# SBUF tiles on 512-byte lines, and constant products ahead of chunk 4's transposes

## The chip, the cores and the metric

The kernel runs on one core of one Trainium2 chip. The metric is the device time of one execution in microseconds; where several runs are shown, their median counts. A core has TensorE (PE; its weight loads are listed as PEld), VectorE (DVE), ScalarE (ACT), GpSimd (POOL) and SyncE (SP), which work in their own order and wait for each other through semaphores. Sixteen DMA engines move data between HBM and SBUF; a transfer is issued by SP, ACT or POOL and stands in that engine's DMA queue.

## The reference, cut to what matters

First a linear attention with decay per head, then a feed-forward layer with a leaky activation:

```python
gamma = 1.0 - 2.0 ** (-5.0 - np.arange(H))            # B=4, H=8, S=768, D=64
for t in range(S):
    state = gamma[None, :, None, None] * state + einsum('bhd,bhe->bhde', k[:, :, t], v[:, :, t])
    y[:, :, t] = scale * einsum('bhd,bhde->bhe', q[:, :, t], state)
x = y.transpose(0, 2, 1, 3).reshape(B * S, H * D)      # 3072 x 512
h = x @ w_in                                           # 512 x 2048
g = maximum(h, 0) + alpha * minimum(h, 0)
out = g @ w_out                                        # 2048 x 512
```

## The kernel before

The recurrence is done in chunks of 128 time steps. A batch has 6 chunks, so there are 24 chunks, numbered u; four chunks make one block of 512 tokens, and there are 6 blocks n. A chunk goes through these steps:

- `load(u)` (line 101): SP issues three transfers, k, q and v of the chunk, 256 KB each, in runs of 256 bytes (64 floats of one head), each into its own SBUF tile. Eight buffers of each.
- `prep(u)`: k times a decay table goes into the fp16 tile kdq (line 119; on DVE for chunks 0 to 7, later on POOL), q times another into its other half (line 127, POOL), and v is cast to fp16 into one of eight tiles vext (line 139, POOL). vext has, for each of four pairs of heads, three blocks of 64 columns: the first head's v, zeros, the second head's v. From chunk 10 on (`NPE`) a DMA transposes kdq into kq.
- `stage_a(u)`: for chunks 0 to 9 PE transposes kdq, eight transposes into the PSUM tile trb (line 156), of which the first four need k and the last four q; ACT copies them to kq (line 163). Unless it is a batch's last chunk, PE makes the state's update stp from kdq and vext (line 169), DVE adds it to the state (line 181, or copies it for a batch's first chunk, line 185), and POOL scales the state into tg (line 187).
- `stage_b(u)`: PE makes the scores sca and scb, pairs of products on 64 rows each (line 202); DVE masks them (line 212).
- `stage_c(u)`: PE makes the outputs yps (lines 227, 234, 242), ACT copies them to xT (line 252), the block's transposed input to the feed-forward layer.

`ffn1(n)` makes 16 products hps of 512 columns (line 270), each of four matmuls, whose activation is done by ACT (line 280) and DVE (line 281); `ffn2(n)` makes the block's outputs ops (line 309), which ACT copies (line 318) and stores. Both are generators: `tick(gen, m)` lets the next m matmuls be issued.

The order on each engine is as the program writes it (`manual_schedule`). Chunks 0 to 3 come first. The weights, w_in in four parts and w_out in four, are issued by POOL in between (lines 348 and 352), with a cast from float32 to fp16. The loads of chunks 4 to 11 are issued by SP once the second part of w_out has landed (`held`). Then `ffn1(0)` runs, then 19 matmuls of `ffn2(0)`, with `prep(4)` before the last nine, and then chunks 4 to 7 are interleaved with the rest of `ffn2(0)`:

```python
    gen = ffn2(0, parts=4)
    tick(gen, 10)
    prep(4)
    tick(gen, 9)
    for u in range(UB, 2 * UB):
        stage_a(u)
        tick(gen, 5)
        if u > UB:
            stage_c(u - 1)
```

Later blocks run `ffn1(n)`, and `ffn2(n)` interleaved with the four chunks of the next block.

PSUM has eight buffers of one bank, four under the tag `pa` (chunks, and every second product of ffn1(0) from the fifth on) and four under `pb`; a tag's buffers are taken in turn. SBUF tiles lie one behind the other in the order in which they are first named: tab, mi, alpha, warm, oma, w_in, w_out, the eight vext, the states, and then those of chunks and blocks.

Of the kernel before, what the change touches and what calls it, by code (L numbers as in the profile page):

```python
# [9 lines left out]
FP = mybir.dt.float32  # L10
F16 = mybir.dt.float16
# [7 lines left out]
def kernel(  # L19
# [10 lines left out]
    nc = tc.nc  # L30
    B, H, S, D = q.shape
    d_model, d_ff = moe_w_in.shape
    NFT = d_ff // 128
    NP = H // 2
# [9 lines left out]

    NTAB = 2 * H + NP + 16
    tab_np = np.zeros((128, NTAB), dtype=np.float64)
    for h in range(H):
        tab_np[:, h] = g64[h] ** (127.0 - p_ar)  # L50
        tab_np[:, H + h] = scale * g64[h] ** (p_ar + 1.0 - 128.0)
    for p in range(NP):
        tab_np[0:64, 2 * H + p] = g64[2 * p] ** 128
        tab_np[64:128, 2 * H + p] = g64[2 * p + 1] ** 128
    tab_np[0:NFT, NTAB - 16 : NTAB] = np.eye(NFT)
    tab_np = tab_np.astype(np.float32)
# [7 lines left out]
    sbp = ctx.enter_context(tc.tile_pool(name="sbp", bufs=1, space=bass.MemoryType.SB))  # L64
    psp = ctx.enter_context(tc.tile_pool(name="psp", bufs=1, space=bass.MemoryType.PSUM))
    ctx.enter_context(tc.manual_schedule())

    tab = sbp.tile([128, NTAB], FP, tag="tab", name="tab")
    mi = sbp.tile([128, 256], F16, tag="mi", name="mi")
    mask = mi[:, 0:128]  # L70
    ident = mi[:, 128:256]
    alpha_sb = sbp.tile([NFT, 128], FP, tag="alpha", name="alpha")
    warm = sbp.tile([128, 1], FP, tag="warm", name="warm")
    oma_sb = sbp.tile([128, NFT], FP, tag="oma", name="oma")
    w_in_all = sbp.tile([128, 4, d_ff], F16, tag="win", name="win")
    w_out_all = sbp.tile([128, NFT, d_model], F16, tag="wout", name="wout")


    NV = 8
    NPE = 10  # L80
    vext = [sbp.tile([128, NP, 3, 64], F16, tag=f"vx{i}", name=f"vx{i}") for i in range(NV)]

    NT = 2
    sst = [sbp.tile([128, NP, 128], FP, tag=f"ss{i}", name=f"ss{i}") for i in range(NT)]
# [2 lines left out]
    def ps(name, dt=FP, n=512, tag="pa"):  # L87
        return psp.tile([128, n], dt, tag=tag, bufs=4, name=name)
# [27 lines left out]
    def prep(u, between=None):  # L116
        t = staged.pop(u)
        kdq = sbp.tile([128, 2, H, D], F16, tag="kdq", bufs=8, name=f"kdq{u}")
        (nc.vector if u < 2 * UB else nc.gpsimd).tensor_tensor(  # L119
            out=kdq[:, 0],  # L120
            in0=t["k"],
            in1=tab[:, 0:H].unsqueeze(2).to_broadcast([128, H, D]),
            op=MULT,
        )
        if between:
            between()
        nc.gpsimd.tensor_tensor(  # L127
            out=kdq[:, 1],
            in0=t["q"],
            in1=tab[:, H : 2 * H].unsqueeze(2).to_broadcast([128, H, D]),  # L130
            op=MULT,
        )
        kq = sbp.tile([128, 2 * NP, 128], F16, tag="kq", bufs=8, name=f"kq{u}")
        if u >= NPE:
            nc.sync.dma_start_transpose(
                out=kq, in_=kdq.rearrange("p a h d -> p (a h d)")
            )
        vx = vext[u % NV]
        nc.gpsimd.tensor_copy(  # L139
            out=vx[:, :, 0::2, :],  # L140
            in_=t["v"].rearrange("p (a b) d -> p a b d", b=2),
        )
        prepped[u] = (kdq, kq, vx)
# [52 lines left out]
    def stage_b(u):  # L196
        kq, vx = live[u]
        scs = [ps("sca"), ps("scb")]
        for p in range(NP):
            for lh in range(2):  # L200
                s = slice(64 * lh, 64 * lh + 64)
                nc.tensor.matmul(  # L202
                    out=scs[lh][:, 128 * p : 128 * p + 128],
                    lhsT=kq[s, 128 * p : 128 * p + 128],
                    rhs=kq[s, 512 + 128 * p : 512 + 128 * p + 128],
                    start=True,
                    stop=True,
                )
        m2s = []
        for lh in range(2):  # L210
            m2 = sbp.tile([128, NP, 128], F16, tag=f"m2{lh}", bufs=2, name=f"m2{lh}")
            nc.vector.tensor_tensor(  # L212
                out=m2,
                in0=scs[lh].rearrange("p (a i) -> p a i", i=128),
                in1=mask.unsqueeze(1).to_broadcast([128, NP, 128]),
                op=MULT,
            )
            m2s.append(m2)
        live[u] = (kq, vx, m2s)

    def stage_c(u):
        b, c = divmod(u, NCH)
        kq, vx, m2s = live.pop(u)
        yps = ps("yps")
        for p in range(NP):
            o = yps[:, 128 * p : 128 * p + 128]
            nc.tensor.matmul(  # L227
                out=o,
                lhsT=vx[:, p, 0:2, :].rearrange("p a d -> p (a d)"),
                rhs=m2s[0][:, p, :],  # L230
                start=True,
                stop=False,
            )
            nc.tensor.matmul(  # L234
                out=o,
                lhsT=vx[:, p, 1:3, :].rearrange("p a d -> p (a d)"),
                rhs=m2s[1][:, p, :],
                start=False,
                stop=(c == 0),
            )  # L240
            if c > 0:
                nc.tensor.matmul(  # L242
                    out=o,
                    lhsT=tgs[u][:, p, :],
                    rhs=kq[:, 512 + 128 * p : 512 + 128 * p + 128],
                    start=False,
                    stop=True,
                )
        n, i = divmod(u, UB)
        if i == 0:  # L250
            xT[n] = sbp.tile([128, NP, TB], F16, tag="xT", bufs=2, name=f"xT{n}")
        nc.scalar.activation(  # L252
            out=xT[n][:, :, C * i : C * i + C],
            in_=yps.rearrange("p (a i) -> p a i", i=128),
            func=COPY,
            bias=0.0,
            scale=1.0,
        )
# [41 lines left out]
    def ffn2(n, parts=1):  # L300
# [3 lines left out]
        for f0 in range(0, NFT, step):  # L304
            for tq in range(UB):
                if f0 == 0:
                    opss[tq] = ps("ops", tag="pb")
                for ft in range(f0, f0 + step):
# [13 lines left out]
                        nc.scalar.dma_start(out=out[row : row + 128, :], in_=os_sb)  # L322
                    yield

    def tick(gen, m):
        for _ in range(m):
            if next(gen, 1) == 1:
                return
# [27 lines left out]
    for u in range(UB):  # L356
# [3 lines left out]
        if u == 0:  # L360
            aps = ps("aps")
            nc.tensor.transpose(
                out=aps[:, 0:NFT], in_=alpha_sb, identity=tab[0:NFT, NTAB - 16 : NTAB]
            )
        stage_b(u)
        if u == 0:
            nc.vector.tensor_scalar(
                out=oma_sb, in0=aps[:, 0:NFT], scalar1=-1.0, scalar2=1.0, op0=MULT, op1=ADD
# [12 lines left out]

    gen = ffn1(0, early=4)
    tick(gen, 8)
    stage_c(UB - 1)
    for _ in gen:
        pass
    gen = ffn2(0, parts=4)
    tick(gen, 10)
    prep(4)
    tick(gen, 9)  # L390
    for u in range(UB, 2 * UB):
        stage_a(u)
        tick(gen, 5)
        if u > UB:
            stage_c(u - 1)
        if u + 1 < 2 * UB:
            prep(u + 1)
        tick(gen, 2)
        stage_b(u)
        tick(gen, 4)  # L400
# [60 lines left out]
```

## Time and profile before

| | us |
|---|---|
| median of three runs | 229.88 |
| lowest and highest | 229.29 and 230.71 |
| profiled execution, first to last instruction (span) | 228.2 |

No device time of the profiled execution stands beside its span; the median is 1.7 us above the span.

| engine | busy us | share of the span |
|---|---|---|
| PE | 209.4 | 92% |
| DVE | 125.1 | 55% |
| PEld | 107.9 | 47% |
| ACT | 96.5 | 42% |
| POOL | 82.7 | 36% |

The mean granted clock of TensorE is 0.981 of full speed. The queue that carries the loads moved 22.55 MB in 89664 packets and took 51.7% of the sixteen DMA engines' span; the weights' queue moved 4.19 MB (as written) and took 11.6%.

How to read it: a page of the profile shows one execution. Busy time is an average over stages with different limits, so a share says little by itself. The slices show when each engine was busy, in tenths. The chain of work that ended last is followed back from the last instruction, each time to what released it; what is not on it costs nothing as long as it stays off. A window gives the same busy times for a stretch of the span. The timeline lists an engine's instructions with their start and duration; what stands in brackets is the idle time before, and who ended it. Matmuls are pipelined, so their durations overlap, and the distance between starts is the better measure.

### The profile page before, as it was taken

How to read it: one execution, taken by the hardware profiler on the slowest of the kernel's cores; microseconds unless marked ns; L12 is line 12 of the kernel's file. 1: busy time of each engine (PE TensorE's matmuls, PEld its weight loads, DVE VectorE, ACT ScalarE, POOL GpSimd, SP SyncE). 2: the span in 40 equal slices, each digit the busy share in tenths (PEclk: the TensorE clock that was granted, in tenths of full speed). 3: DMA queues.
4: the chain of work that ended last, by engine and by line, in shares of the span. 5: the costliest groups of instructions: out<-in, count | busy, mean ns of one | idle time of the engine just before them, and what ended most of it. 6: DMA issues, size and time to landing. Idle time of an engine off the chain costs nothing.

```text
span 228.2 us, 3703 instructions
## 1 busy us (share of the span) xinstructions
PE 209.4 (92%) x1409; PEld 107.9 (47%) x1409; DVE 125.1 (55%) x202; ACT 96.5 (42%) x156; POOL 82.7 (36%) x98
## 2 busy tenths in 40 slices
PE   1697999299989999999999999999999999999992
PEld 0475644146544555544455544455544455544441
DVE  3485595155438855338864268943288834288100
ACT  2243673024657732166522266423376222567121
POOL 2689400254796034950031990103970130000000
PEclk9999999769999999999999999999999999999998
DMA  7999999999999998599911399971371011200111
GB/s 154 218 195 142 206 187 204 205 233 204 248 297 233 212 187 216 126 254 229 219 51 46 82 220 211 194 176 46 92 158 29 0 46 61 79 0 0 49 64 74
DMA packets 97681, 33.36 MB, mean 146 GB/s; under 512 B 90352, under 2 KB 94592, under 8 KB 97664
## 3 DMA queue, kind: packets, MB, share of 16 engines
q1 hardware_dynamic: 89664, 22.55, 51.7%
q0 software_dynamic: 4224, 4.19, 11.6%
q10 hardware_dynamic: 3776, 6.39, 7.8%
q8 instruction: 11, 0.18, 0.3%
q14 instruction: 6, 0.05, 0.1%
HBM read 27.36 MB, written 6.29 MB: 147 GB/s over the span
## 4 chain that ended last, share of the span: by engine, by line
PE 76%; DMA 11%; POOL 6%; SPq 3%; issue 1%; DVE 1%; ACT 1%; POOLq 0%; DVEq 0%
PE ops L309 34%; PE hps L270 30%; DMA qs<-in_q_dram 6%; DMA wout<-in_moe_w_out_dram 5%; SPq L101 3%; PE sca L202 3%; POOL tg L187 2%; PE yps L234 2%; PE yps L227 2%; POOL kdq L127 2%; PE stp L169 2%; PE yps L242 2%; POOL win L348 1%; PE trb L156 1%; POOL vx L139 1%
## 5 line engine op out<-in xcount | busy, mean ns | idle before, releaser
L309 PE MATMUL ops<-wout,gt 128*128 128x512 f16 x384 | 94.2, 384 | 0.0
L281 DVE SCALAR_TENSOR_TENSOR gt<-hm,oma,hps 128x512 f16<-128x512 f32 x96 | 70.7, 747 | 34.0 <-ACT hm L280 25.1
L270 PE MATMUL hps<-xT,win 128*128 128x512 f16 (+2 forms) x400 | 84.2, 370 | 1.9 <-DMA win<-in_moe_w_in_dram 1.4
L280 ACT ACTIVATE hm<-hps 128x512 f32<-128x512 f32 x96 | 57.0, 597 | 25.1 <-PE hps L270 24.7
L270 PEld LDWEIGHTS <-win 128*128 128x128 f16 x400 | 38.3, 98 | 46.4 <-DMA win<-in_moe_w_in_dram 1.6
L309 PEld LDWEIGHTS <-gt 128*128 128x128 f16 x384 | 34.8, 99 | 34.9 <-issue 1.4
L187 POOL TENSOR_TENSOR tg<-ss,tab 128x512 f16<-128x512 f32 x20 | 21.6, 1082 | 77.3 <-DVE ss L181 54.1
L127 POOL TENSOR_TENSOR kdq<-qs,tab 128x512 f16<-128x512 f32 x24 | 25.0, 1042 | 26.4 <-DMA qs<-in_q_dram 26.3
L212 DVE TENSOR_TENSOR m<-sca,mi 128x512 f16<-128x512 f32 x24 | 16.6, 692 | 28.6 <-PE scb L202 28.4
L318 ACT ACTIVATE os<-ops 128x512 f32<-128x512 f32 x24 | 14.3, 596 | 39.6 <-PE ops L309 39.5
L252 ACT ACTIVATE xT<-yps 128x512 f16<-128x512 f32 x24 | 14.3, 597 | 34.1 <-PE yps L242 29.2
L163 ACT ACTIVATE kq<-trb 128x1024 f16<-128x1024 f16 x10 | 10.2, 1023 | 27.3 <-PE trb L156 26.8
L156 PE MATMUL trb<-mi,kdq 128*128 128x128 f16 x80 | 9.0, 263 | 11.7 <-DVE kdq L119 8.9
L181 DVE TENSOR_TENSOR ss<-tg,stp 64x256 f32<-64x256 f16 x32 | 13.4, 418 | 9.6 <-PE stp L169 8.5
L234 PE MATMUL yps<-m,vx 128*128 128x128 f16 x96 | 17.6, 227 | 0.4 <-DVE m L212 0.4
L227 PE MATMUL yps<-m,vx 128*128 128x128 f16 x96 | 17.6, 227 | 0.0
L119 POOL TENSOR_TENSOR kdq<-ks,tab 128x512 f16<-128x512 f32 x16 | 16.7, 1042 | 0.4 <-DMA ks<-in_k_dram 0.4
L212 DVE TENSOR_TENSOR m<-scb,mi 128x512 f16<-128x512 f32 x24 | 16.3, 681 | 0.0
L242 PE MATMUL yps<-kq,tg 128*128 128x128 f16 x80 | 14.9, 224 | 0.0
L139 POOL CAST vx<-vs 128x512 f16<-128x512 f32 x24 | 14.6, 609 | 0.7
L156 PEld LDWEIGHTS <-kdq 128*128 128x128 f16 x80 | 6.2, 114 | 15.2 <-DVE kdq L119 9.4
L119 DVE TENSOR_TENSOR kdq<-ks,tab 128x512 f16<-128x512 f32 x8 | 6.1, 764 | 12.5 <-DMA ks<-in_k_dram 12.5
(23 smaller groups left out, 83.1 us busy)
## 6 DMA issues: line engine op xcount, KB each, us to landing
ks<-in_k_dram SPq DMA_DIRECT2D x24, 256.0 KB, 4.6
qs<-in_q_dram SPq DMA_DIRECT2D x24, 256.0 KB, 4.8
vs<-in_v_dram SPq DMA_DIRECT2D x24, 256.0 KB, 5.0
out_dram<-os ACTq DMA_DIRECT2D x24, 256.0 KB, 2.0
win<-in_moe_w_in_dram POOLq DMA_DIRECT2D x4, 512.0 KB, 6.4
wout<-in_moe_w_out_dram POOLq DMA_DIRECT2D x4, 512.0 KB, 13.2
kq<-kdq SPq DMA_TRANSPOSE x14, 4.1
mi<-mi_const ACTq DMA_DIRECT2D x1, 64.0 KB, 3.3
```

What stands on the lines that cost most here:

```text
L119: (nc.vector if u < 2 * UB else nc.gpsimd).tensor_tensor(out=kdq[:, 0], in0=t["k"], in1=tab[:, 0:H].unsqueeze(2).to_broadcast([128, H, D]) ...
L127: nc.gpsimd.tensor_tensor(out=kdq[:, 1], in0=t["q"], in1=tab[:, H : 2 * H].unsqueeze(2).to_broadcast([128, H, D]), op=MULT,)
L156: nc.tensor.transpose(out=trb[:, 128 * p : 128 * p + 128], in_=kdq[:, p // NP, 2 * (p % NP) : 2 * (p % NP) + 2, :].rearrange("p a d -> p ( ...
L187: nc.gpsimd.tensor_tensor(out=tg, in0=new, in1=tab[:, 2 * H : 2 * H + NP].unsqueeze(2).to_broadcast([128, NP, 128]), op=MULT,)
L212: nc.vector.tensor_tensor(out=m2, in0=scs[lh].rearrange("p (a i) -> p a i", i=128), in1=mask.unsqueeze(1).to_broadcast([128, NP, 128]), op ...
L227: nc.tensor.matmul(out=o, lhsT=vx[:, p, 0:2, :].rearrange("p a d -> p (a d)"), rhs=m2s[0][:, p, :], start=True, stop=False,)
L234: nc.tensor.matmul(out=o, lhsT=vx[:, p, 1:3, :].rearrange("p a d -> p (a d)"), rhs=m2s[1][:, p, :], start=False, stop=(c == 0),)
L242: nc.tensor.matmul(out=o, lhsT=tgs[u][:, p, :], rhs=kq[:, 512 + 128 * p : 512 + 128 * p + 128], start=False, stop=True,)
L270: nc.tensor.matmul(out=hpss[ft][:, lo:hi], lhsT=w_in_all[:, hp, 128 * ft : 128 * ft + 128], rhs=xT[n][:, hp, lo:hi], start=(hp == 0), stop ...
L280: nc.scalar.activation(out=hm, in_=hps, func=RELU, bias=0.0, scale=-1.0)
L281: nc.vector.scalar_tensor_tensor(out=gt[:, ft, :], in0=hm, scalar=oma_sb[:, ft : ft + 1], in1=hps, op0=MULT, op1=ADD,)
L309: nc.tensor.matmul(out=opss[tq], lhsT=gt[:, ft, 128 * tq : 128 * tq + 128], rhs=w_out_all[:, ft, :], start=(ft == 0), stop=(ft == NFT - 1),)
```

## The change

Two things are done. First, four tiles are made longer, and nothing is put into the added part: tab has 96 columns in place of 36, warm and oma have 128 in place of 1 and 16, and each vext has a fourth block of 64 columns per pair of heads, so that its first three blocks are used through a view. With the four constants of 32 bytes that lie ahead of them, every tile from mi on then begins at a multiple of 512 bytes. Second, `keep_busy` is called between the 19th matmul of `ffn2(0)` and `stage_a(4)`. It takes two PSUM buffers of the tag `pa` and issues 64 matmuls from the constant tile mi (the mask and the identity) into them; nothing reads the result. `rows` picks 64 or all 128 rows of mi, `cols` the 64 PSUM partitions that are written, n is 128 or 64 columns.

```diff
-    NTAB = 2 * H + NP + 16
+    NTAB = 96
...
-    warm = sbp.tile([128, 1], FP, tag="warm", name="warm")
-    oma_sb = sbp.tile([128, NFT], FP, tag="oma", name="oma")
+    warm = sbp.tile([128, 128], FP, tag="warm", name="warm")[:, 0:1]
+    oma_sb = sbp.tile([128, 128], FP, tag="oma", name="oma")[:, 0:NFT]
...
-    vext = [sbp.tile([128, NP, 3, 64], F16, tag=f"vx{i}", name=f"vx{i}") for i in range(NV)]
+    vext = [
+        sbp.tile([128, NP, 4, 64], F16, tag=f"vx{i}", name=f"vx{i}")[:, :, 0:3, :]
+        for i in range(NV)
+    ]
...
+    def keep_busy():
+        t0, t1 = ps("idle0"), ps("idle1")
+
+        def one(rows, cols, bank, at, n, w):
+            nc.tensor.matmul(
+                out=bank[cols, at : at + n],
+                lhsT=mi[rows, w : w + (cols.stop - cols.start)],
+                rhs=mi[rows, 0:n],
+                start=True,
+                stop=True,
+            )
+
+        lo, hi, al = slice(0, 64), slice(64, 128), slice(0, 128)
+        for i in range(8):
+            one(al, lo, t0, 128 * (i % 4), 128, 64 * (i % 2))
+            one(al, hi, t0, 128 * (i % 4), 128, 64 * (i % 2))
+        for i in range(4):
+            one(lo, lo, t0, 128 * i, 128, 64 * (i % 2))
+            one(hi, hi, t0, 128 * i, 128, 64 * (i % 2))
+            one(lo, hi, t1, 128 * i, 128, 64 * (i % 2))
+            one(hi, lo, t1, 128 * i, 128, 64 * (i % 2))
+        for i in range(4):
+            one(lo, lo, t0, 64 * i, 64, 64 * (i % 2))
+            one(hi, hi, t0, 64 * i, 64, 64 * (i % 2))
+            one(lo, hi, t1, 64 * i, 64, 64 * (i % 2))
+            one(hi, lo, t1, 64 * i, 64, 64 * (i % 2))
+        for i in range(4):
+            one(lo, lo, t0, 128 * i, 128, 64 * (i % 2))
+            one(hi, hi, t0, 128 * i, 128, 64 * (i % 2))
+        for i in range(4):
+            one(al, lo, t0, 64 * i, 64, 64 * (i % 2))
+            one(al, hi, t0, 64 * i, 64, 64 * (i % 2))
...
     prep(4)
     tick(gen, 9)
+    keep_busy()
     for u in range(UB, 2 * UB):
```

## The prediction

> **What bounds the kernel now.** I read the page's slices first, then the chain of work that ended last, then the windows and the timeline around the one hole that TensorE has. The slices:
>
> ```profile
> PE   1697999299989999999999999999999999999992
> ...
> POOL 2689400254796034950031990103970130000000
> PEclk9999999769999999999999999999999999999998
> DMA  7999999999999998599911399971371011200111
> ```
>
> A slice is 5.7 us. From the ninth on PE is full. Before that, DMA is full and PE has holes; the clock row dips in the eighth and ninth slices. So only the first 50 us can give something away, and what is saved there shows at the end. The chain of waits there (start, length):
>
> ```profile
> 23.25 12.32 DMA wout<-in_moe_w_out_dram
> 35.59 0.37 SPq L101
> 36.00 8.01 DMA qs<-in_q_dram
> 44.08 1.05 POOL kdq L127
> 45.18 0.61 PE trb L156 x4
> 45.78 0.56 PE stp L169 x4
> 46.34 2.94 PE ops L309 x7
> ```
>
> The weights come in for 12 us on the chain, then chunk 4's q for 8, then POOL scales it, and PE goes on. The last line is the odd one: seven products in 2.94 us, where the same chain has 1.51 for seven at 79.53. The windows tell why (length, busy time of PE, PEld, DVE, ACT, POOL, then the granted clock, the share and GB/s of DMA):
>
> ```profile
> 14.97:18.38 3.41, 3.27 (x34) 2.73 (x33) 2.88 (x5) 1.33 (x2) 3.39 (x5) 1.00 0.82 116
> 18.38:21.80 3.42, 1.88 (x27) 1.35 (x27) 2.27 (x5) 1.61 (x2) 3.42 (x5) 1.00 1.10 159
> 38.86:42.28 3.42, 1.34 (x7) 0.39 (x4) 0.00 (x0) 0.00 (x0) 0.00 (x0) 1.00 1.25 245
> 42.28:45.69 3.41, 1.12 (x8) 0.79 (x9) 0.69 (x1) 0.00 (x0) 1.61 (x2) 0.50 0.80 164
> 45.69:49.10 3.41, 3.41 (x12) 1.26 (x10) 1.53 (x3) 1.02 (x1) 1.63 (x3) 0.50 1.23 239
> ```
>
> The granted clock is 0.50 from 42.28 to 49.10 us, that is 6.83 us, two equal stretches of 3.41. I cut the trace into stretches of that length from there: one in which PE was 39% busy (1.34 of 3.42) lost the clock, one with 55% kept it, one that was full gave it back. And the engines between:
>
> ```profile
> 44.08 1.04 POOL L127 TENSOR_TENSOR kdq<-qs,tab 128x512 f16<-128x512 f32 x1 [18.59 <-DMA qs<-in_q_dram]
> ...
> 45.09 0.61 POOL L139 CAST vx<-vs 128x512 f16<-128x512 f32 x1
> ...
> 46.45 0.87 DVE L181 TENSOR_TENSOR ss<-tg,stp 64x256 f32<-64x256 f16 x2 [2.42 <-PE stp L169]
> ...
> 47.49 1.45 POOL L187 TENSOR_TENSOR tg<-ss,tab 128x512 f16<-128x512 f32 x1 [1.78 <-DVE ss L181]
> ...
> 48.90 1.04 POOL L127 TENSOR_TENSOR kdq<-qs,tab 128x512 f16<-128x512 f32 x1
> ...
> 50.41 0.61 PE L156 MATMUL trb<-mi,kdq 128*128 128x128 f16 x8
> ```
>
> POOL has no pause from 47.49 to its kdq for chunk 5 (to 49.94); PE arrives at that chunk's transposes at 50.41. POOL is less than half a microsecond from being the bound.
>
> **The products ahead of chunk 4.** 64 matmuls with their weight loads, on PE alone, after the 19th ffn2 product (ends 40.2) and before chunk 4's transposes (44.08, waiting 3.88 us for DVE's kdq). Each is 128 or 64 columns wide. The nearest row is the sca/scb pairs on two 64-row halves: pairs start at 49.21, 49.28, 49.33, 49.39, so 57 ns a pair. 32 pairs are 1.8 us. A change of tile shape costs about 0.1 (two ops from 52.61 at 0.216 each end 53.04; the pairs start 53.14); four changes are 0.4. So 2.2 us, to 42.4. If no two run together, 64 x 57 ns is 3.65, with 0.4 more it ends at 44.25: the first half of the transposes slips by 0.17, but the second half waits for POOL until 45.18 anyway. All of it is covered by the hole; without that cover it would cost its 2.2 to 4.1 us whole. Their two PSUM buffers held ffn1's products 8 and 10, whose last reader, DVE, ends the whole of ffn1 at 37.51; the chunk's own buffers then come from products 12 and 14, also free. Behind them in PE's queue stand only the transposes. No DMA queue is touched.
>
> What it buys is the clock after 44.08, if it holds. The second half of the transposes stays at 45.18 (POOL). stp needs POOL's cast of v, which ends at 45.70: 45.72 against 45.76, and at full clock it takes 0.39 (the stp at 54.79) instead of 0.58, so it ends 0.23 earlier. Seven ops take 1.51, so sca comes at 47.5 instead of 49.21: 1.7 earlier. But that is not the gain. Late next is POOL: ss, tg and kdq of chunk 5 only move by the 0.23, so kdq ends at 49.71. PE reaches the second half of chunk 5's transposes at 48.9 and waits for 49.76, against 50.63 before (50.41 plus half of 0.45). Gain 0.87. It carries on: chunk 6's kdq (51.51, waits for its q, ends 52.55) stays ahead of its transposes (54.34 less 0.87), and the row tg, kdq, vx from 56.33 starts with a stp and so moves with it. From 65 us PE has no idle time to swallow it.
>
> **The lines of 512 bytes.** By the tiles' sizes in order (four constants of 32 bytes, tab 144 padded to 160, mi 512, alpha 512, warm 32, oma 64) every tile from win on starts 128 bytes past a 256-byte line and 384 past a 512-byte one; with the change all start on both. For engines I take nothing: no group's work changes in elements; vx goes from a pair step of 384 bytes to 512, with the same runs of 64. If the cast cost 10% more (61 of 609 ns), chunk 4's stp would be 0.06 late. tab is 48 KB instead of 18; its packets of 144 bytes took 14 ns, those of 512 took 27, so 8 a engine are at most 0.1 us longer, and the first user waits for k until 4.25 anyway.
>
> What could move is DMA. In the trace's packet records a 256-byte packet of q, k or v takes 18 ns, one of 512 (mi) 27, of 144 (tab) 14, of 2048 (output) 84: some 8.5 ns fixed and 1.17 per 32 bytes. All of these start off a 256-byte line, so the records can't say what an aligned one takes. Half of the 256-byte packets cross a 512-byte line and half don't; both take 18, so that line alone costs nothing. Bounds by rows: nothing, or 3 ns a packet (the first of an engine took 15; the 64-byte instruction packets 8, where the fit gives 10.8). A loss has no row that speaks for it. I take nothing, because one straight line fits four sizes that start at three different offsets.
>
> The Trainium skill, "DMA: Bandwidth & Descriptors", section "How a descriptor splits into AXI transactions", says that a descriptor off a 256-byte line still pays for the bytes from the line below, for reads. Applied to writes that would be 12 beats instead of 8, an estimate of 4.7 ns of the 18. The 18 ns agree with it, the 27 ns of the 512-byte packets are longer than it gives; by it the rival below would come out at 226.6.
>
> **Sum.** The profiled execution spans 228.2; the median of the runs is 229.88, so 1.7 lie around it, taken as unchanged. 228.2 - 0.87 + 1.7 = 229.0.
>
> **Rivals.** (a) *The clock drops anyway.* Products to 42.4, then idle to 44.08 and again to 45.18: a stretch of 3.41 us that starts between 41.1 and 42.9 is under 45% busy, between the 39% that lost the clock and the 55% that kept it. The profiled one starts at 42.28, inside. Then half clock would come at 45.69 and end at 49.10, as before, and only the 0.2 to 0.3 us of transposes and stp stay: 229.6. Against it: where the stretches fall need not be the same in each execution, and 41.1 to 42.9 is half of 3.41. The skill's "TensorE: Matmul & The Clock Gate", section "What's actually happening", has the clock drop after an idle window; here one that was 39% busy lost it, so the trace differs, and by the page alone this rival would be out.
>
> (b) *Aligned packets are shorter.* With 3 of 18 ns saved, the first twelve loads (768 packets an engine, back to back at 217 to 221 GB/s until 16 us) pass faster; chunk 2's q, the eighth, lands 512 x 3 ns = 1.5 us sooner, POOL, which waits for it until 12.94, issues the weights that much sooner, and the whole train to 44.08 follows. With chunk 4's own loads 1.7, and 0.87 for the clock: 227.3. It is 228.0 if the clock drops all the same, and 226.5 if the weights' packets (98 ns, 256 an engine) get 3 ns shorter too, 0.8 us. For it: DMA is full to 44 us. Against: the straight line above.
>
> (c) *Slower: the products outlast the hole.* At full clock the work from the transposes to sca takes 2.3 us, and sca stands at 49.21, so it decides when they end after 46.9, 6.7 us or 105 ns each. Weight loads last 98 ns (PEld rows); if none hides behind a product, 98 + 56 = 154 ns, 9.9 us, end 50.1, sca 3.2 later: 233.1. Against it: the pairs at 57 ns. The skill's "TensorEngine Tiling (Array Packing)" says, under "Key Properties" and "Restrictions", that a change of mode drains the array and that column tiles do without fast weight load. No row has column tiles; the first part agrees with the 0.1 us gap. An estimate from the weight-load rule of the clock page (64 columns at 1.2 per ns, 53 ns, none hidden) is 109 ns each and 230.2.
>
> **How the numbers follow.** Forecast (clock held, DMA unmoved) 0.36; (a) 0.22; (b) 0.35; (c) 0.07. The likeliest alone: 228.4 to 229.9, its 229.0 with the spread of the three runs, some 0.7. The range must reach into (b) and leave (c) out: 226.5 to 230.4. A measurement tells about 1%, 2.3 us, from no change: faster than 227.6 is two thirds of (b), 0.23, and a little of the forecast, 0.27 together; slower than 232.2 is most of (c), 0.06; within, 0.67.
>
> **What would show it.** Clock row: 1.00 through 42 to 49 us (forecast), a 0.50 from 45.7 (a). PE waiting for POOL's kdq of chunk 5 some 0.8 us (forecast). 256-byte packets at 18 ns, chunk 4's DVE kdq at 43.3 (forecast); 14 or 15 ns and 41 to 42 us (b). The products over in 1.4 to 4.1 us; more than 6.7 is (c). The forecast is wrong if the first twelve loads run above 230 GB/s, or if PE idles on something new after 50 us.

## The result and the profile after

The changed kernel takes 227.26 us (median of four runs, 227.12 to 227.42); the kernel before, run beside it, 229.92. One run of the kernel before, beside later kernels, took 1201 us; it counts as slow and is left out of every comparison. The ratio is 0.9879, interval 0.9854 to 0.9905: 2.7 us or 1.2% faster. That lies in the stated range, 1.7 us below the point of 229.0, and a hair from what rival (b) gave, 227.3.

The profiled execution spans 225.3 us, 2.9 less than before. Its slices, to be held against those of before:

```profile
PE   1686999589899999999999999999999999999992
...
POOL 3699300285784026930123980114960220000000
PEclk9999999999999999999999999999999999999999
DMA  7989999999999993999711399941760021100111
```

The dip of the clock row is gone. The chain before, in the stretch ahead of the weights:

```profile
7.72 5.15 DMA qs<-in_q_dram
...
12.94 1.04 POOL kdq L127
...
15.74 0.88 POOL win L348
```

The chain after, from there to chunk 4's q:

```profile
7.34 4.33 DMA qs<-in_q_dram
...
11.73 1.16 POOL kdq L130
...
14.53 0.88 POOL win L384
...
22.05 11.65 DMA wout<-in_moe_w_out_dram
33.72 0.37 SPq L104
34.13 7.82 DMA qs<-in_q_dram
42.02 1.04 POOL kdq L130
```

It has the same links in the same order. POOL scales chunk 2's q 1.21 us earlier (11.73 against 12.94) and issues the weights that much earlier, and chunk 4's q is scaled 2.06 us earlier (44.08 before). Two quantities settle the time, and I use them for every kernel below: when POOL scales chunk 4's q (the *head*), and how long it is from there to the first matmul of the second block's ffn1 (the *middle*, 20.81 us before: 44.08 to 64.89). Behind that nothing changes in this pair: from the second block's ffn1 to the end it is 163.3 us before (228.2 less 64.89) and after (225.3 less 61.97). After, head 42.02 and middle 19.95. So 2.06 us came from the head and 0.86 from the middle.

The middle first, in the timeline after (start, length, engine):

```profile
38.89 1.57 PE L332 MATMUL idle<-mi 128*64 128x128 f16 x64
...
41.96 0.40 PE L159 MATMUL trb<-mi,kdq 128*128 128x128 f16 x4 [1.49 <-DVE kdq L122]
...
45.20 1.45 POOL L190 TENSOR_TENSOR tg<-ss,tab 128x512 f16<-128x512 f32 x1 [1.58 <-DVE ss L184]
...
46.62 1.04 POOL L130 TENSOR_TENSOR kdq<-qs,tab 128x512 f16<-128x512 f32 x1
...
47.71 0.40 PE L159 MATMUL trb<-mi,kdq 128*128 128x128 f16 x4 [0.62 <-POOL kdq L130]
```

The 64 products take 1.57 us and end well before chunk 4's k is there. At chunk 5 PE waits 0.62 us for POOL's kdq: the new bound that the prediction named, in its place.

The head, in the windows from 2 to 17 us, before and then after (the last two columns are the share and GB/s of DMA):

```profile
2.00:17.00 15.00, 9.22 (x81) 6.75 (x81) 8.22 (x16) 5.46 (x7) 8.20 (x10) 1.00 1.25 214
```

```profile
2.00:17.00 15.00, 9.05 (x89) 6.78 (x90) 9.64 (x18) 5.78 (x8) 9.50 (x12) 1.00 0.98 218
```

The engines of DMA are less busy and move no less: PE got through 89 matmuls in place of 81, since the twelve loads are over at 15.8 instead of 16.9 us. The queue table of the page says the same for the whole span, at equal packets and bytes; before and after:

```profile
q1 hardware_dynamic: 89664, 22.55, 51.7%
```

```profile
q1 hardware_dynamic: 89664, 22.55, 47.4%
```

In the packet records the most frequent 256-byte packet still takes 18 ns. What has gone are the longer ones: before, 22% of the packets of the first 17 us took 18 ns or less and 48% more than 24; after, all take 18 or less. The mean went from 23.9 to 17.9 ns.

### The profile page after: what moved, and what is told of

It reads as the page before. It is cut to its first block, busy times and chain, and to the rows that moved or that the text cites. A ratio compares the mean times of both kernels' runs of the same rounds, so it can differ in the third digit from the quotient of the medians.

```text
span 225.3 us, 3831 instructions
## 1 busy us (share of the span) xinstructions
PE 207.7 (92%) x1473; PEld 107.7 (48%) x1473; DVE 125.6 (56%) x202; ACT 96.6 (43%) x156; POOL 83.2 (37%) x98
## 3 DMA queue, kind: packets, MB, share of 16 engines
q1 hardware_dynamic: 89664, 22.55, 47.4%
## 4 chain that ended last, share of the span: by engine, by line
PE 74%; DMA 11%; POOL 7%; SPq 3%; DVE 1%; issue 1%; ACT 1%; POOLq 0%; DVEq 0%
PE ops L312 33%; PE hps L273 31%; DMA qs<-in_q_dram 5%; DMA wout<-in_moe_w_out_dram 5%; SPq L104 3%; POOL tg L190 3%; PE sca L205 3%; POOL kdq L130 2%; PE yps L237 2%; PE yps L230 2%; PE stp L172 2%; PE yps L245 2%; POOL win L384 1%; POOL vx L142 1%; PE trb L159 1%
## 5 line engine op out<-in xcount | busy, mean ns | idle before, releaser
L312 PE MATMUL ops<-wout,gt 128*128 128x512 f16 x384 | 92.7, 380 | 0.0
L215 DVE TENSOR_TENSOR m<-sca,mi 128x512 f16<-128x512 f32 x24 | 16.6, 692 | 27.5 <-PE scb L205 27.3
L166 ACT ACTIVATE kq<-trb 128x1024 f16<-128x1024 f16 x10 | 10.2, 1023 | 24.5 <-PE trb L159 24.1
L237 PE MATMUL yps<-m,vx 128*128 128x128 f16 x96 | 17.0, 223 | 0.4 <-DVE m L215 0.4
L159 PE MATMUL trb<-mi,kdq 128*128 128x128 f16 x80 | 8.3, 246 | 9.8 <-DVE kdq L122 6.1
L230 PE MATMUL yps<-m,vx 128*128 128x128 f16 x96 | 17.1, 223 | 0.0
L142 POOL CAST vx<-vs 128x512 f16<-128x512 f32 x24 | 15.1, 630 | 0.5 <-DMA vs<-in_v_dram 0.5
L245 PE MATMUL yps<-kq,tg 128*128 128x128 f16 x80 | 14.4, 219 | 0.0
L122 DVE TENSOR_TENSOR kdq<-ks,tab 128x512 f16<-128x512 f32 x8 | 6.7, 837 | 10.2 <-DMA ks<-in_k_dram 10.1
```

What stands on the lines that cost most here:

```text
L122: (nc.vector if u < 2 * UB else nc.gpsimd).tensor_tensor(out=kdq[:, 0], in0=t["k"], in1=tab[:, 0:H].unsqueeze(2).to_broadcast([128, H, D]) ...
L142: nc.gpsimd.tensor_copy(out=vx[:, :, 0::2, :], in_=t["v"].rearrange("p (a b) d -> p a b d", b=2),)
L215: nc.vector.tensor_tensor(out=m2, in0=scs[lh].rearrange("p (a i) -> p a i", i=128), in1=mask.unsqueeze(1).to_broadcast([128, NP, 128]), op ...
L230: nc.tensor.matmul(out=o, lhsT=vx[:, p, 0:2, :].rearrange("p a d -> p (a d)"), rhs=m2s[0][:, p, :], start=True, stop=False,)
L237: nc.tensor.matmul(out=o, lhsT=vx[:, p, 1:3, :].rearrange("p a d -> p (a d)"), rhs=m2s[1][:, p, :], start=False, stop=(c == 0),)
L245: nc.tensor.matmul(out=o, lhsT=tgs[u][:, p, :], rhs=kq[:, 512 + 128 * p : 512 + 128 * p + 128], start=False, stop=True,)
```

## The experiments

Two theories stood against each other. Theory 1: a 256-byte packet that starts off a line of 256 bytes makes DMA slower, which sets the head; the products hold the clock, which sets the middle; and the two add. Theory 2: the layout moves nothing, and the head came earlier because full clock was granted at 14 us instead of 18, by the trace's clock records. In this part a packet's time is the mean of the 256-byte packets that start in the first 17 us. The ratios are to the kernel before, run beside each.

**Each part alone.**

```diff
 e1, from the kernel after:
-    keep_busy()
     for u in range(UB, 2 * UB):
 e2, from the kernel before:
     tick(gen, 9)
+    keep_busy()
     for u in range(UB, 2 * UB):
```

Lines only:

> The longer tiles alone, without the 64 products. Theory 1 (lines of 256 bytes: off such a line the q, k and v packets get in each other's way, 23.9 ns mean in the first 17 us against 17.9; on it a load takes 1.11 us instead of 1.20): the packets stay at 17.9, chunk 4's q is scaled at 42.0 instead of 44.1, the half clock is back after the hole, and the time is about 2.0 below before, 227.9. Theory 2 (layout moves nothing; the head came earlier because the clock was granted at 14 us instead of 18): packets 17.9 or not, chunk 4's q at 44.1 and 229.9.

Measured: 227.83 us, ratio 0.991 (0.9882 to 0.9937). Packets 18.0 ns, head 41.86, middle 20.65 with the clock at half from 43.17 to 46.59. Theory 1 to the letter.

Products only:

> The 64 products alone, tiles laid as before (384 bytes past a line of 512). Theory 1: packets at 23.9 ns, chunk 4's q at 44.1, clock held, PE waits some 0.6 us for POOL's kdq of chunk 5: 229.0, that is 0.9 below before; the two parts alone add to the 2.7 of both. Theory 2: all of the gain, 227.3. If the clock drops at 45.7 all the same: 229.6.

Measured: 229.68 us, ratio 0.999 (0.9963 to 1.0016), not to be told from no change. Packets 24.1 ns, clock held in the hole. Head and middle mislead here: the head was 43.03, 1.05 us earlier than in the profile of before with the same packets, and the middle 21.08 in spite of the clock, for a reason that I had not thought of:

```profile
45.15 0.61 POOL L139 CAST vx<-vs 128x512 f16<-128x512 f32 x1 [1.08 <-DMA vs<-in_v_dram]
45.81 0.38 PE L169 MATMUL stp<-vx,kdq 128*128 128x128 f16 x4 [1.29 <-POOL vx L139]
```

POOL and behind it PE wait for chunk 4's v, the load behind q. Its cast starts at 45.15, and at 45.09 in the profile of before, so the wait took what the early head had given, not what the clock gave: from the cast to the second ffn1 it is 18.97 us here and 19.80 before. Theory 2 is out: this kernel has the products and none of the loads' gain, and e1 has that gain without them. The chains leave no place for it either: in none of the traces does the chain hold work of PE between 7 us and the head, and POOL scales chunk 2's q at 12.8 to 12.9 us in the kernels off the line and at 11.3 to 11.7 in those on it. The record of full clock starts at 17.7 to 19.3 us off the line and at 11.4 to 16.6 on it, so it goes with the layout, but it sets nothing on that chain.

**Which line.**

```diff
 e3 / e4 / e7, from the kernel after:
-    NTAB = 96
+    NTAB = 160     # e3: tiles 256 bytes past a line of 512
+    NTAB = 64      # e4: 384 past, as before
+    NTAB = 104     # e7: 32 past
```

> The whole change, but the first table is 256 bytes longer, so that all tiles start on a line of 256 bytes and off one of 512. Theory 1: no difference to the whole change, 227.3, packets 17.9 ns. Rival (the line that counts is 512 bytes): half of the 256-byte packets, or all of the 1024-byte and 2048-byte ones, start off a line; the mean packet goes up towards 24 ns and the time to 228 to 229.

Measured: 227.51 us, ratio 0.9893 (0.987 to 0.9915), packets 18.0 ns. A line of 256 bytes is enough, within the intervals. (In its profile the head is 43.00, since the weights came in late; the middle is 19.95.)

> The whole change, but the first table is 128 bytes shorter, so that all tiles from the mask on start 384 bytes past a line of 512, as most did before. Theory 1: packets at 23.9 ns again, chunk 4's q at 44.1, 229.0, as with the 64 products alone. Theory 2, or if the longer v tiles themselves are what helped: 227.3.

Measured: 229.19 us, ratio 0.9972 (0.9947 to 0.9996), packets 24.1 ns, head 43.33, middle 20.28 with 0.5 us of waiting for chunk 4's v. With the longer tiles and the products, but off the line, most of the gain is gone.

> The whole change with all tiles 32 bytes past a line of 512. If any start off a 256-byte line costs the same, since a packet is cut in two either way: 24 ns mean and 229.2. If the cost goes with the bytes that lie beyond the line (128 of 256 before, 32 of 256 here): some 20 ns and 227.8. If lines of less than 256 bytes matter too (all tiles were on lines of 128 before): more than 24 ns and over 229.5.

Measured: 230.25 us, ratio 1.0009 (0.9991 to 1.0027), packets 24.8 ns, a load in 1.20 us, head 43.70. So 32 bytes past the line cost at least what 128 do, and the cost does not go with the bytes beyond it. That fits a packet that is cut in two, but no run shows the cut itself. Time and packets also meet what was expected if lines of less than 256 bytes matter too: the time is above e4's by 1.1 us. The profile lost the clock (45.04 to 48.46, middle 20.71), which explains some half of a microsecond. Whether the small offset costs something of its own stays open.

**Which tiles.** An unused tile ahead of the q, k and v tiles and another behind them shift these alone:

```diff
 e5, from the kernel after (e6: NTAB = 64, pad0 of 32 and pad1 of 96 columns):
     sst = [...]
+    pad0 = sbp.tile([128, 96], FP, tag="pad0", name="pad0")
...
         t = staged.pop(u)
+        if u == 0:
+            pads.append(sbp.tile([128, 32], FP, tag="pad1", name="pad1"))
```

> The whole change, but the q, k and v tiles alone lie 384 bytes past a line of 512 again; everything else stays on lines. Theory 1a (the gain is in the twelve loads at the start and the four behind the weights, through their 256-byte packets): the mean packet of the first 17 us is 24 ns, a load takes 1.20 us, the time is 229.2 as with all tiles off. Theory 1b (the weights, or the kdq, kq and output tiles, carry part of it): between 227.3 and 229.2.

> The reverse: the q, k and v tiles on lines of 512 bytes, everything else 384 bytes past one. Theory 1a: packets of the first 17 us at 18 ns, a load in 1.06 us, and 227.3 as with the whole change. Theory 1b: 228 to 229.

Measured: loads off 229.62 us, ratio 0.998 (0.9962 to 0.9999), packets 23.4 ns; loads on, all else off, 227.38 us, ratio 0.9886 (0.9859 to 0.9913), packets 18.0. Loads off, then loads on, in the window from 2 to 17 us:

```profile
2.00:17.00 15.00, 9.38 (x81) 6.78 (x82) 8.27 (x16) 5.62 (x7) 8.36 (x10) 1.00 1.23 216
```

```profile
2.00:17.00 15.00, 9.05 (x98) 6.61 (x99) 9.74 (x18) 6.35 (x8) 9.95 (x12) 1.00 1.02 224
```

Within the intervals (some 0.6 us either way) the q, k and v tiles carry all of it, and where the weights, kdq, kq and the outputs lie makes no difference that can be told.

**The clock.** Products issued twice (`keep_busy()` on two lines):

> The whole change with the 64 products issued twice, 3.1 us in place of 1.57, ending about when chunk 4's kdq is there. If the products buy the clock and the whole change sometimes still loses it, the clock is never 0.50 between 40 and 60 us and the time is 227.0 with less spread; if they buy it fully already, 227.3; if doubled products delay the transposes, up to 227.6.

Measured: 227.09 us (226.93 to 227.52), ratio 0.9871 (0.9853 to 0.9889), middle 19.94, clock held; the time is not to be told from that of the whole change. Its stretch with the hole is 86% busy:

```profile
39.05:42.46 3.41, 2.94 (x124) 2.28 (x118) 0.69 (x1) 0.00 (x0) 0.47 (x1) 1.00 0.91 201
```

Products of whole tiles:

```diff
 e10, the body of keep_busy:
+        al = slice(0, 128)
+        for i in range(28):
+            one(al, al, t0 if i < 14 else t1, 128 * (i % 4), 128, 128 * (i % 2))
```

> The whole change with 28 products of the full 128 x 128 tile and 128 columns in place of the 64 in four shapes; at the 56 ns of such products that is the same 1.57 us of PE. If only busy time counts for the clock: 227.3, and from chunk 4's kdq to the next ffn1 19.95 us where the clock holds. If the shapes matter (small tiles fill the array less, or a change of shape costs): the clock holds in other cases than with the mixed ones, and the products' time is not 1.6 us; 227.0 to 227.8 either way.

Measured: 227.63 us, ratio 0.9892 (0.9852 to 0.9932); the runs lie between 227.03 and 229.69. In the profiled one the clock dropped all the same, and the middle is 20.82. Its stretches:

```profile
40.47:43.88 3.41, 0.84 (x10) 0.51 (x9) 0.69 (x1) 0.12 (x1) 1.59 (x2) 1.00 0.89 201
43.88:47.30 3.42, 3.42 (x11) 1.29 (x10) 1.53 (x3) 0.91 (x1) 1.69 (x2) 0.50 1.09 247
```

The shape need not explain it: the products ended at 40.5, just as this stretch began, so that it was only 25% busy. e6, with the mixed shapes, lost the clock too, after a stretch that was 45% busy:

```profile
38.70:42.11 3.41, 1.53 (x60) 1.07 (x54) 0.69 (x1) 0.00 (x0) 0.44 (x1) 1.00 0.97 218
42.11:45.53 3.42, 2.76 (x13) 1.54 (x14) 1.46 (x3) 1.02 (x1) 1.64 (x3) 0.50 1.11 252
```

Profiles are single executions, but every run has its mean granted clock on record. One stretch of 3.41 us at half clock lowers it by some 0.0075 (half of 3.41 out of 227). In 50 runs without the products (44 of before, 6 of e1) it is never above 0.993. With the products once it is 0.996 or more in 12 of 58 runs, and with them twice (e8, e9) in 10 of 10. So the products issued once keep the clock throughout in about a fifth of the runs, and issued twice in all that were taken. Where in a run the clock was lost these means don't say.

**Past the new bound.** POOL is now the one that PE waits for at chunk 5, so its order was changed:

```diff
 e9, from e8:
     for u in range(UB, 2 * UB):
+        if u + 1 < 2 * UB:
+            prep(u + 1)
         stage_a(u)
         tick(gen, 5)
         if u > UB:
             stage_c(u - 1)
-        if u + 1 < 2 * UB:
-            prep(u + 1)
```

> Tiles on lines, the 64 products issued twice, and in chunks 4 to 7 prep(u + 1) moved ahead of stage_a(u), so that POOL scales the next chunk's q before this chunk's state and not after. Theory 1 says that with the clock held POOL is the bound at chunk 5's transposes (PE waits 0.62 us for its kdq); then this wait goes, kdq of chunk 5 follows its q's landing at about 44.8, and the time is 226.2 to 226.5. If the engines now stand behind a load instead (DVE's kdq in front of the state's addition, POOL's in front of tg): 227.1, no change, with PE waiting for DVE's ss or POOL's tg.

Measured: 226.85 us, ratio 0.985 (0.9821 to 0.9878): the fastest here, though its interval meets that of the whole change. PE's wait at chunk 5 is gone, and in the profiled run the second ffn1 starts at 60.96, 0.97 earlier than with e8. Behind that all of it is lost again, since both profiled runs span 225.2 us: the chain shows ACT held until a load of k has landed at 63.1, ahead of its store, and PE waits 0.82 us for ffn1's activations, a wait that the whole change and e8 don't have there. Why ACT's store stands behind that load the trace doesn't say. So the new order trades one wait for another.

All profiles in one table (us; the column before the last is from the start of chunk 4's v cast to the second block's ffn1, the last where the clock was at half between 40 and 50 us):

| kernel | loads on a 256-byte line | 256-byte packet, ns | weights' first packet | head | middle | v cast to ffn1 | half clock |
|---|---|---|---|---|---|---|---|
| before | no | 23.9 | 17.38 | 44.08 | 20.81 | 19.80 | 42.3 to 49.1 |
| e2 products only | no | 24.1 | 17.22 | 43.03 | 21.08 | 18.97 | no |
| e4 off 128 | no | 24.1 | 17.15 | 43.33 | 20.28 | 18.96 | no |
| e5 loads off | no | 23.4 | 17.19 | 43.76 | 19.95 | 18.95 | no |
| e7 off 32 | no | 24.8 | 17.17 | 43.70 | 20.71 | 19.64 | 45.0 to 48.5 |
| after | yes | 17.9 | 16.12 | 42.02 | 19.95 | 18.96 | no |
| e1 lines only | yes | 18.0 | 15.76 | 41.86 | 20.65 | 19.66 | 43.2 to 46.6 |
| e3 off 256 | yes | 18.0 | 15.75 | 43.00 | 19.95 | 18.95 | no |
| e6 loads on | yes | 18.0 | 15.55 | 41.67 | 20.22 | 19.23 | 42.1 to 45.5 |
| e8 twice | yes | 18.0 | 15.79 | 41.99 | 19.94 | 18.95 | no |
| e9 prep first | yes | 18.0 | 16.02 | 42.25 | 18.71 | 17.72 | no |
| e10 whole tiles | yes | 18.0 | 16.11 | 42.23 | 20.82 | 19.83 | 43.9 to 47.3 |

The column from v's cast separates the two effects best: in the order of before it is 18.95 to 18.97 in all six profiles that kept the clock here, with either layout, and 19.23 to 19.83 in the five that lost it.

## Why the prediction came out as it did

*The step that failed* is "I take nothing" for DMA. I took the most frequent packet, 18 ns in the first profile, as the price of a packet, fitted a line through four sizes and concluded that the start of a packet costs nothing. The line fits those four most frequent times, and with aligned tiles the most frequent packet is still one of 18 ns. But before, only 22% of the packets of the first 17 us took 18 ns or less, so "both take 18" was not what the records said, and I passed over the mean. The page's queue row gives it (51.7% of sixteen engines' 228.2 us over 89664 packets is 21 ns), and a DMA share above one (1.25 from 2 to 17 us) said that packets overlapped. The loads went through at 1.20 to 1.21 us each; aligned they take 1.02 to 1.11 (nine loads, from the second's to the eleventh's last packet, in all kernels of the table). The weights' first packet, which waits for POOL and so for these loads, comes at 17.2 us on average in the five kernels off the line and some 1.4 us earlier, at 15.9, in the seven on it. From there to the head it is 26.4 and 26.3 us, so the weights gain nothing, as e6 also shows. In the one pair that was profiled first it was 0.8 less (26.7 and 25.9); among the aligned kernels alone it lies between 25.9 and 27.3, so that part of the 2.06 can be chance from execution to execution. A little more may come at chunk 4's v, for which PE waits 1.3 and 0.5 us in e2 and e4; its cast starts at 44.9 us on average off the line and at 43.1 on it, 1.7 us earlier.

*Rival (b)* had the size and the place: 1.5 us at the weights and 227.3 in all. It had the wrong mechanism, 3 ns off each packet. The shortest did not get shorter; the long ones went. So the agreement in size is partly luck, and the time lies in the stated range because that was made to reach into (b), not because the forecast's sum held: it had nothing for the loads. What happens inside a DMA engine no run shows. The Trainium skill, "DMA: Bandwidth & Descriptors", section "How a descriptor splits into AXI transactions", names the line of 256 bytes, for reads. Applied to writes, it gives an estimate of 4.7 ns less for each aligned packet (put in place of rival (b)'s 3 ns, that makes 226.4, not 226.6). The runs bear out the line but not this estimate, since the most frequent packet stayed at 18 ns.

*The 512-byte line* costs nothing by itself that can be told, as the prediction said: e3.

*The middle* is the step that came out nearly to the digit: forecast gain 0.87 us, measured 0.86 (20.81 to 19.95), with stp, ss, tg and kdq of chunk 5 as the chain and PE's new wait of 0.62 (forecast: 0.8). The seven products got 1.5 us faster and the kernel only 0.9, because POOL had been only 0.5 us from being the bound.

*Rival (a)*, the clock drops anyway, is not a rival but a share of the executions. It happened over the hole in e6, e7 and e10, and not in after, e2, e3, e4 and e5. My bounds for it held (though a stretch under 45% busy would have had to start after 41.3, not 41.1): in the stretches of 3.41 us from 17 us on, the clock went after one that was 18, 25, 26, 39 or 45% busy, and stayed after 52, 53, 55, 57 or 60% or more; between lie two at 48 and 49% that lost it (e2 and e4, at 18 us, which put ffn1 at half clock from 21 to 25 us and the products at 41.9) and one at 49% that kept it (e9). So the limit is about half. The Trainium skill's "TensorE: Matmul & The Clock Gate", section "What's actually happening", lets an idle window do this. The runs here show that a window that is less than half busy is enough. Doubled products keep each stretch over the hole above 75% in its profile. The spread of the runs tells less than the clocks on record: 0.3 us for the whole change and 0.6 for e8, but 2.0 for e6, 1.6 for e9 and 2.4 for e1.

*Rival (c)* was wrong in its price: 64 products last 1.57 us, not 9.9, and also less than my 2.2, since four quadrants run together and not two, and a product of 64 columns takes less than one of 128.

What the products are worth by the runs: with lines, 227.83 without and 227.26 with them, 0.57; without lines, 230.04 and 229.68. Neither difference alone is beyond the intervals. Both are below the 0.86 us of the middle, which rest on the profiles; that fits products that keep the clock in a part of the runs only. The two parts alone, 2.2 and 0.4, add to nearly the 2.7 of both; by the profiles they are 1.7 (the start of v's cast, on average) and 0.84 (from there to ffn1, before and after). So how the gain is divided is known to about half a microsecond only.

## What to carry to other kernels

Look at the mean of a DMA packet and at a share above one, not at the most frequent packet alone: there the slow loads showed. Put the tiles that many short runs are written to on a line of 256 bytes; here it cost a few bytes of padding, and only those tiles mattered. Before pricing a wait that goes, follow who is next: here POOL's work took back nearly half of what the clock gave. Check that what is to keep the clock does so in every run: issued once the products did not, issued twice they did.

## What was not expected of the hardware

Of the 64 products, pairs on two column halves (128 x 64) start 4 ns apart and the next pair about 55 ns later, like the pairs on row halves. The four quadrants (64 x 64) start within 10 ns of each other and take about 55 ns for 128 columns each, and about 31 ns for 64. Going from column halves to quadrants takes 149 ns between starts, and back 146. So what looked like 64 products is 24 steps. And the clock stayed full on stretches of 3.41 us that were only a little over half busy (52 to 60% above).
